# Reading the moving columns of the float32r matmuls from two halves in turn, in a convolution and feed-forward kernel

## The chip, the cores and the metric

The kernel runs on one core of one Trainium2 chip. The metric is the device time of one execution in microseconds (us). A core has five engines with queues of their own: TensorE (PE; its weight loads are shown apart as PEld), VectorE (DVE), ScalarE (ACT), GpSimd (POOL) and SyncE (SP). PE reads its operands from SBUF and adds its results up in PSUM; ACT and DVE read PSUM.

## The reference

A causal convolution of 7 taps along the sequence, with one softmax-normalized set of taps for each of 8 groups of 24 channels, then a feed-forward layer:

```python
w = softmax(weight)                       # (8 heads, 7 taps)
out[b, s, h, g] = sum_k w[h, k] * x_pad[b, s + k, h, g]   # x: (8, 4096, 192), 6 zeros in front
x = out.reshape(32768, 192)
h = x @ w_in                              # (192, 2048)
g = where(h >= 1, h, where(h <= -1, 0, (h + 1)**2 / 4))
return g @ w_out                          # (2048, 192)
```

Everything is float32, and the result has float32 precision.

## The kernel before

The 32,768 tokens go in 64 blocks of 512, numbered from 0. `d_ff` goes in 8 pairs of two 128-wide slices. A unit `q` is one pair of one block, so there are 512 units; `s, j = divmod(q, 8)`. Channels and `d_ff` stand on partitions, tokens in the free dimension.

For each unit PE first runs the products of `mm1` (line 440): the activations are the moving operand (512 tokens), the weights the stationary one, and the sum `h` (two PSUM banks of 512 tokens) has the tokens in the order of the moving columns. ACT then makes relu and square (lines 552, 553), DVE the min and max against `h` (line 878), and ACT a rounded copy `gh` in float32r (line 563); DVE makes the rest `gl = g - gh` and the sum `gt` of its two slices (lines 569, 575). Three units later PE runs `mm2` (line 501), with `gh`, `gl` and `gt` as the moving operand, into four PSUM banks `accr0`, `accr1`, `accm0`, `accm1`, which add up over the 8 units of a block.

Block 0 uses float32 for both layers; block 1 uses float32r for the first layer and float32 for the second (`mm2_first`, line 473, where `g` is the stationary operand). From block 2 on, both layers are made of three float32r products each (high times high, low times high, high times low). The very last unit is float32 again in its second layer (`pair_last`, line 650).

The contraction is cut into 64-row halves. Every product is issued as two matmuls, one on partitions 0 to 63 and one on 64 to 127, which run beside each other. A float32r unit has 9 such pairs in `mm1` and 9 in `mm2`, 36 matmuls of 64 rows x 512 columns.

At the end of a block `evac_banks` (line 593) copies the four banks to SBUF on ACT (line 599), in the order `accr0`, `accr1`, `accm0`, `accm1`. Each bank has one buffer, so the next block's `mm2` cannot start in a bank before its copy is done. Adding the four copies (`evac_add`, POOL's DMA queue, line 608), a transpose on DVE and the stores (`store`, line 610, SP's queue) follow later. The last block has its own copies (`evac_last`, line 635), split over ACT and DVE in halves of 256 tokens.

The order of the work on every engine is the order of the code: the schedule is written out by hand, in the main loop at the end of the function.

Of the kernel before, what the change touches and what calls it, by code (L numbers as in the profile page):

```python
# [8 lines left out]
F32 = mybir.dt.float32  # L9
# [9 lines left out]
P = 128  # L19
TB = 512  # L20
# [11 lines left out]
def lightconv_then_ffn(ctx: ExitStack, tc: tile.TileContext, x, weight, w_in, w_out, out):  # L32
# [24 lines left out]
    nc = tc.nc  # L57
    B, S, D = x.shape
# [11 lines left out]
    HALVES = (TOP, BOT)  # L70
# [6 lines left out]
    ob = ctx.enter_context(tc.tile_pool(name="ob", bufs=2))  # L77
# [359 lines left out]
    NQ = NSB * NPAIR  # L437
    hs, g32, gs, ghs, gls, gts, accs = {}, {}, {}, {}, {}, {}, {}

    def mm1(q):  # L440

        s, j = divmod(q, NPAIR)

        if q == 0:
            h = hs[q] = [ps_o.tile([P, TB], F32, name=n) for n in ("accr1", "accm0")]
        else:
            h = hs[q] = ps_h.tile([P, 2, TB], F32, name="h")
            h = [h[:, e, :] for e in range(2)]

        if q == 0:  # L450
            for e in range(2):
                nc.tensor.matmul(h[e], natural[:, e * P:(e + 1) * P], xop[s]["all"],  # L452
                                 start=True, stop=False)
            for e, half in enumerate(HALVES):
                nc.tensor.matmul(h[e], natural[half, CW:CI], xop[s]["r"][e],  # L455
                                 start=False, stop=True)
            return
        if s == 0:
            mms = [(WI[j], u + u, [xop[s][u]] * 2) for u in "nrs"]
        else:  # L460
            mms = [(W[j][:, part], u + u, [xop[s][u, x]] * 2) for u in "nsr"
                   for part, x in ((0, "hi"), (1, "hi"), (0, "lo"))]
        for n, (w, us, x) in enumerate(mms):
            for e in range(2):
                c0 = COL[us[e]][e]
                nc.tensor.matmul(h[e], w[HALVES[e], c0:c0 + P], x[e][e],  # L466
                                 start=(n == 0), stop=(n == len(mms) - 1))

    def new_accs(s):
        accs[s] = {(a, i): ps_o.tile([P, TB], F32, name=f"acc{a}{i}")  # L470
                   for a in "mr" for i in range(2)}

    def mm2_first(q):


        s, j = divmod(q, NPAIR)
        g, w = g32.pop(q), WF[j + LAG]
        if j == 0:
            new_accs(s)
        for e in range(2):  # L480
            for b in range(TB // P):
                a, c0 = "mr"[b // 2], b % 2 * D
                for i, half in enumerate(HALVES):
                    nc.tensor.matmul(accs[s][a, i][:, c0:c0 + D], g[half, e, b * P:(b + 1) * P],  # L484
                                     w[half, e, :], start=(j == 0 and e == 0 and b % 2 == 0),
                                     stop=(j == NPAIR - 1 and e == 1 and b % 2 == 1))

    XY, XZ, ZY = range(3)
# [5 lines left out]
    def leave(mm):  # L494
        nc.tensor.drain(fusable=True).then_inc(turns, 1)
        turn[0] += 1

    def enter():
        nc.tensor.wait_ge(turns, turn[0])

    def mm2(q):

        s, j = divmod(q, NPAIR)
        gh, gl, gt = ghs.pop(q), gls.pop(q), gts.pop(q)
        if j == 0:
            new_accs(s)
        wg, wl = WG[j], WL[j]
        low = {XY: gt, XZ: gl[:, 1, :], ZY: gl[:, 0, :]}
        seen = set()
        for k in range(9):  # L510
            for i, half in enumerate(HALVES):
                turned = k // 3 if j % 2 == 0 else 2 - k // 3
                bank, part = BANKS[i][turned], PARTS_OF[i][turned]
                w, g = ((wg[:, k % 3, part], gh[:, k % 3, :]) if k % 3 < 2
                        else (wl[:, part], low[part]))
                if i == 0 and k == 6:
                    enter()
                mm = nc.tensor.matmul(accs[s][bank], w[half], g[half],  # L518
                                      start=(j == 0 and bank not in seen),
                                      stop=(j == NPAIR - 1 and k % 3 == 2  # L520
                                            and (bank[0] == "m" or k == 8)
                                            or q == NQ - 2 and k % 3 == 2
                                            and (bank[0] == "m" or k == 8)))
                seen.add(bank)
                if i == 1 and k == 3:
                    leave(mm)
# [67 lines left out]
    def evac_banks(s):  # L594
        acc = accs.pop(s)
        t = {}
        for bank in (("r", 0), ("r", 1), ("m", 0), ("m", 1)):
            t[bank] = ob.tile([P, TB], F32, name="t", bufs=4)
            nc.scalar.copy(t[bank], acc[bank])
        sums[s, "m"], sums[s, "r"] = t["m", 0], t["r", 0]  # L600
        sums[s] = t

# [30 lines left out]
    last = {}  # L633

    def evac_last(s):

        acc = accs.pop(s)
        half, rest = slice(0, TB // 2), slice(TB // 2, TB)
        u, v, r = [ob.tile([P, TB], F32, name="t", bufs=4) for _ in range(3)]
        for n in (half, rest):  # L640
            nc.scalar.copy(u[:, n], acc["m", 0][:, n])
            nc.vector.tensor_tensor(out=v[:, n], in0=acc["m", 1][:, n], in1=u[:, n], op=ALU.add)
        for n in (half, rest):
            for to, a in ((TOP, 0), (BOT, 1)):
                nc.vector.tensor_tensor(out=v[to, n], in0=acc["r", a][to, n], in1=v[to, n],
                                        op=ALU.add)
                nc.scalar.copy(r[to, n], acc["r", 1 - a][to, n])
        last["m"], last["r"] = v, r

    def pair_last(q):  # L650

# [303 lines left out]
    for q in range(NQ + LATE):  # L955
        s, j = divmod(q, NPAIR)
        c, i = divmod(q, 2 * NPAIR)
# [8 lines left out]
        if c == 0 and i in (4, 5, 10):  # L966
            u = {4: "a", 5: "r", 10: "b"}[i]
# [7 lines left out]
        if q == NPAIR:  # L975
            mm2_first(done)
        if q < NQ:
            mm1(q)
        if done is not None and q != NPAIR:
            (pair_last if done == NQ - 1 else mm2 if done >= NF32 else mm2_first)(done)  # L980
# [21 lines left out]
        else:  # L1002
# [4 lines left out]
            if done is not None and done % NPAIR == NPAIR - 1 and done < NQ - 1:  # L1007
                (evac if done < NF32 else evac_banks)(done // NPAIR)
            if done == NQ - 2:
                evac_last(done // NPAIR)  # L1010
            if q == NF32:
                parts_lo(q)
            n = q - 1 if q < NF32 + 3 else q - 2
# [14 lines left out]
            if q < NQ:  # L1028
                if s > 2 and j in (3, 4):
                    evac_add(s - 1, j - 3)  # L1030
                if s <= 2 or s == NSB - 1:
                    m = 6 if s > 2 else 2
# [43 lines left out]
```

## Time and profile before

| | |
|---|---|
| device time, median of 3 runs | 2121.58 us (2121.57 to 2122.2) |
| profiled execution, first to last instruction (span) | 2120.2 us |
| PE busy | 2115.9 us (100% of the span) |
| ACT busy | 1976.6 us (93%) |
| DVE busy | 1975.6 us (93%) |
| POOL busy | 792.4 us (37%) |
| granted TensorE clock, mean over the span | 1.000 (of 2.4 GHz) |

The run times are some 1.4 us longer than the span, since they hold what lies around the first and the last instruction. Busy times of engines overlap. A matmul's row lasts from its start to the end of its last result, so rows of successive matmuls overlap; the rate of PE is read from the distance between starts.

### The profile page before, as it was taken

To read this page: it belongs to the slowest core of one execution; us is meant where nothing else is said; L and a number is where in the kernel's file an instruction comes from. 1 tells how busy PE (TensorE), PEld (TensorE's weight loads), DVE (VectorE), ACT (ScalarE), POOL (GpSimd) and SP (SyncE) were. 2 spreads that over 40 slices of the span, in tenths; PEclk is the share of its full clock that TensorE was granted. 3 is DMA by queue.
4 is the path that set the end of the run, shared out by engine and by line. 5 is a ranking of instruction groups with operands and counts; after the bars stand their busy time and mean duration, and the time that the engine had idled before them with its cause. 6 is when DMAs were issued, how large, how long until landed. Compare 5 with 4: busy or idle time off the path is not lost.

```text
span 2120.2 us, 46902 instructions
## 1 busy us (share of the span) xinstructions
PE 2115.9 (100%) x18644; PEld 1807.7 (85%) x18644; DVE 1975.6 (93%) x2109; ACT 1976.6 (93%) x2381; POOL 792.4 (37%) x749
## 2 busy tenths in 40 slices
PE   9999999999999999999999999999999999999999
PEld 6988888888888888888888888888888888888888
DVE  8899999999999999999999999999999999999997
ACT  7899999999999999999999999999999999999997
POOL 1534333343433433333333333343343333433331
PEclk9999999999999999999999999999999999999999
DMA  6333333433433434334333343343343433433322
GB/s 172 77 66 71 57 73 67 79 73 54 82 66 71 78 63 73 69 64 85 70 60 72 68 79 74 54 81 64 74 76 63 76 68 64 84 68 62 70 54 51
DMA packets 470685, 152.27 MB, mean 72 GB/s; under 512 B 418944, under 2 KB 426624, under 8 KB 470464
## 3 DMA queue, kind: packets, MB, share of 16 engines
q1 hardware_dynamic: 446880, 109.17, 24.7%
q0 software_dynamic: 23424, 39.99, 12.9%
q8 instruction: 146, 2.39, 0.5%
q14 instruction: 75, 0.61, 0.1%
q10 hardware_dynamic: 160, 0.10, 0.0%
HBM read 32.84 MB, written 25.17 MB: 27 GB/s over the span
## 4 chain that ended last, share of the span: by engine, by line
PE 100%; DVE 0%; issue 0%; POOL 0%; POOLq 0%; DVEq 0%
PE h L466 49%; PE accr L518 32%; PE accm L518 16%; PE accm L484 1%; PE accr L484 1%; PE accr L214 0%; PE accm L721 0%; PE accm L193 0%; PE h L664 0%; PE accm L664 0%; PE h L171 0%; PE accr L452 0%; PE accr L455 0%; PE accr L767 0%; PE accm L452 0%; PE accm L171 0%
## 5 line engine op out<-in xcount | busy, mean ns | idle before, releaser
L569 DVE TENSOR_TENSOR gl<-g,gh 128x1024 fp32r<-128x1024 f32 x495 | 742.8, 1501 | 63.4 <-ACT gh L563 58.5
L466 PE MATMUL h<-hi,w 64*128 64x512 f32 x4032 | 629.9, 387 | 0.0
L518 PE MATMUL accr<-gh,wg 64*128 64x512 f32 x3960 | 616.5, 386 | 0.0
L878 DVE SCALAR_TENSOR_TENSOR g<-g,h 128x1024 f32<-128x1024 f32 x504 | 607.8, 1206 | 6.9 <-ACT g L553 5.0
L552 ACT ACTIVATE g<-h 128x1024 f32<-128x1024 f32 (+1 forms) x497 | 509.9, 1026 | 99.5 <-PE h L466 97.4
L553 ACT ACTIVATE g<-g 128x1024 f32<-128x1024 f32 (+1 forms) x497 | 527.4, 1061 | 15.8
L563 ACT CAST gh<-g 128x1024 fp32r<-128x1024 f32 x495 | 516.7, 1044 | 0.5 <-DVE g L878 0.4
L129 POOL TENSOR_TENSOR y<-y,p 128x512 f32<-128x512 f32 x180 | 233.5, 1297 | 607.2 <-ACT p L237 413.0
L466 PEld LDWEIGHTS h<-hi,w 64*128 64x128 f32 x4032 | 391.8, 184 | 64.7 <-DVE g L878 0.2
L518 PEld LDWEIGHTS accr<-gh,wg 64*128 64x128 f32 x3960 | 384.2, 184 | 64.6
L129 POOL TENSOR_TENSOR r<-r,p 128x512 f32<-128x512 f32 x180 | 233.6, 1298 | 510.4 <-ACT p L237 363.7
L466 PE MATMUL h<-lo,w 64*128 64x512 f32 x2016 | 399.9, 386 | 0.0
L518 PE MATMUL accr<-gl,words 64*128 64x512 f32 x1980 | 392.1, 386 | 0.0
L575 DVE TENSOR_TENSOR m<-gl 128x512 fp32r<-128x512 f32 x495 | 336.1, 679 | 20.5 <-DVE gl L569 0.5
L518 PE MATMUL accm<-gh,wg 64*128 64x512 f32 x1980 | 308.3, 386 | 0.0
L466 PE MATMUL h<-rhi,w 64*128 64x512 f32 x992 | 303.9, 386 | 0.0
L466 PE MATMUL h<-rh,w 64*128 64x512 f32 x992 | 303.9, 386 | 0.0
L608 POOL DMA_DIRECT2D t<-t x244 | 206.3, 985 | 93.1 <-DMA t<-t 69.9
L466 PEld LDWEIGHTS h<-lo,w 64*128 64x128 f32 x2016 | 196.2, 184 | 32.3
L518 PEld LDWEIGHTS accr<-gl,words 64*128 64x128 f32 x1980 | 192.1, 184 | 32.3
L518 PEld LDWEIGHTS accm<-gh,wg 64*128 64x128 f32 x1980 | 192.1, 184 | 32.3
L466 PEld LDWEIGHTS h<-rhi,w 64*128 64x128 f32 x992 | 182.5, 184 | 16.2
(161 smaller groups left out, 2322.2 us busy)
## 6 DMA issues: line engine op xcount, KB each, us to landing
t<-t POOLq DMA_DIRECT2D x183, 128.0 KB, 3.7
out_dram<-osb SPq DMA_DIRECT2D x366, 64.0 KB, 1.9
raw<-in_x_dram SPq DMA_DIRECT2D x334, 68.0 KB, 2.4
hi<-hi SPq DMA_DIRECT2D x128, 128.0 KB, 2.8
lo<-lo SPq DMA_DIRECT2D x126, 128.0 KB, 3.1
t<-t POOLq DMA_DIRECT2D x61, 256.0 KB, 3.3
rhi<-rh SPq DMA_DIRECT2D x62, 128.0 KB, 3.5
rlo<-rl SPq DMA_DIRECT2D x62, 128.0 KB, 2.4
```

The lines of the kernel that those rows point to most:

```text
L129: add = nc.gpsimd.tensor_add(out, a, b)
L466: nc.tensor.matmul(h[e], w[HALVES[e], c0:c0 + P], x[e][e], start=(n == 0), stop=(n == len(mms) - 1))
L484: nc.tensor.matmul(accs[s][a, i][:, c0:c0 + D], g[half, e, b * P:(b + 1) * P], w[half, e, :], start=(j == 0 and e == 0 and b % 2 == 0), st ...
L518: mm = nc.tensor.matmul(accs[s][bank], w[half], g[half], start=(j == 0 and bank not in seen), stop=(j == NPAIR - 1 and k % 3 == 2 and (ban ...
L552: nc.scalar.activation(g[:, e, :], hs[q][:, e, :], AF.Relu, bias=0.5, scale=0.5)
L553: nc.scalar.activation(g[:, e, :], g[:, e, :], AF.Square)
L563: nc.scalar.copy(gh[:, e, :], gs[q][:, e, :])
L569: nc.vector.tensor_sub(gl[:, e, :], g[:, e, :], gh[:, e, :])
L575: return nc.vector.tensor_add(gt, gl[:, 0, :], gl[:, 1, :])
L608: nc.gpsimd.dma_start(out=to, in_=src, accum_op=ALU.add)
L878: nc.vector.scalar_tensor_tensor(out=g, in0=g, scalar=1.0, in1=h, op0=ALU.min, op1=ALU.max)
```

## The change

In `mm1` (blocks 1 to 63, but for the last unit) and in `mm2` the moving operand's access pattern is `p (a b) -> p b a` with `a=2`: the columns are read as 0, 256, 1, 257, and so on. A matmul still has 512 columns and writes its 512 results side by side. So `h` holds token `256 a + b` at place `2 b + a`; `gh`, `gl` and `gt` keep that order, and `mm2` applies the same reading once more. In the four banks a place `4 r + 2 b + a` then holds token `256 b + 128 a + r`.

The copies put the tokens back: for `accr0` and `accm0` ACT reads PSUM with a step of four elements and writes side by side; for `accr1` and `accm1` it reads side by side and writes to four places 128 elements apart in turn. `evac_last` reads the banks with a step of four elements on ACT and DVE. In block 1 the second layer takes its stationary blocks of `g` with a step of two elements.

```diff
+    def in_turn(t):
+        return t.rearrange("p (a b) -> p b a", a=2)
+    def by_token(t):
+        return t.rearrange("p (r b a) -> p b a r", b=2, a=2)
     def mm1(q):
+        seen = (lambda t: t) if s == 0 or q == NQ - 1 else in_turn
...
-                nc.tensor.matmul(h[e], w[HALVES[e], c0:c0 + P], x[e][e],
+                nc.tensor.matmul(h[e], w[HALVES[e], c0:c0 + P], seen(x[e][e]),
     def mm2_first(q):
...
-                    nc.tensor.matmul(accs[s][a, i][:, c0:c0 + D], g[half, e, b * P:(b + 1) * P],
-                                     w[half, e, :], start=(j == 0 and e == 0 and b % 2 == 0),
+                    block = (g[half, e, b * P:(b + 1) * P] if s == 0 else
+                             g[half, e].rearrange("p (k i a) -> p k a i", k=2, a=2)[:, b % 2, b // 2])
+                    nc.tensor.matmul(accs[s][a, i][:, c0:c0 + D], block, w[half, e, :], start=(j == 0 and e == 0 and b % 2 == 0),
     def mm2(q):
...
-                mm = nc.tensor.matmul(accs[s][bank], w[half], g[half],
+                mm = nc.tensor.matmul(accs[s][bank], w[half], in_turn(g[half]),
     def evac_banks(s):
...
-            nc.scalar.copy(t[bank], acc[bank])
+            if bank[1] == 0:
+                nc.scalar.copy(t[bank].rearrange("p (b a r) -> p b a r", b=2, a=2),
+                               by_token(acc[bank]))
+            else:
+                nc.scalar.copy(t[bank].rearrange("p (b a r) -> p r b a", b=2, a=2),
+                               acc[bank].rearrange("p (r b a) -> p r b a", b=2, a=2))
     def evac_last(s):
-        half, rest = slice(0, TB // 2), slice(TB // 2, TB)
-        u, v, r = [ob.tile([P, TB], F32, name="t", bufs=4) for _ in range(3)]
-        for n in (half, rest):
+        parts = [ob.tile([P, TB], F32, name="t", bufs=4) for _ in range(3)]
+        u, v, r = [t.rearrange("p (b a r) -> p b a r", b=2, a=2) for t in parts]
+        acc = {k: by_token(t) for k, t in acc.items()}
+        for n in range(2):
...
```

No engine issues an instruction more or less, and none changes its place. What differs is the shape of every second copy. ACT's queue at the end of block 2, before (`t` is the copy in SBUF, `acc..` the PSUM banks, `h` and `g` the tiles of the unit beside it):

```order
L552 ACTIVATE g_1740<-h_1701 128x1024
L553 ACTIVATE g_1740<-g_1740 128x1024
L599 COPY t_1743<-accr0_1329 128x512
L599 COPY t_1745<-accr1_1330 128x512
L599 COPY t_1747<-accm0_1327 128x512
L599 COPY t_1749<-accm1_1328 128x512
L563 CAST gh_1756<-g_1687 128x1024
```

The same place in the changed kernel:

```order
L562 ACTIVATE g_1740<-h_1701 128x1024
L563 ACTIVATE g_1740<-g_1740 128x1024
L610 COPY t_1743<-accr0_1329 128x512
L613 COPY t_1745<-accr1_1330 128x128x4
L610 COPY t_1747<-accm0_1327 128x512
L613 COPY t_1749<-accm1_1328 128x128x4
L573 CAST gh_1756<-g_1687 128x1024
```

Only line numbers and the written shape of `accr1` and `accm1` differ; the four copies stand where they stood, ahead of the next unit's rounded copy.

## Rows read from the trace of the kernel before

**Rows 1.** The page: busy us of each engine, and the chain that ended last.

```profile
PE 2115.9 (100%) x18644; PEld 1807.7 (85%) x18644; DVE 1975.6 (93%) x2109; ACT 1976.6 (93%) x2381; POOL 792.4 (37%) x749
...
PE 100%; DVE 0%; issue 0%; POOL 0%; POOLq 0%; DVEq 0%
```

**Rows 2.** Engines' busy us (and instructions) in 16 units: us, PE, PEld, DVE, ACT, POOL.

```profile
500.00:565.28 65.28, 65.28 (x578) 55.87 (x576) 61.28 (x64) 61.70 (x75) 24.86 (x22) 1.00 0.39 71
1000.00:1065.28 65.28, 65.28 (x578) 55.87 (x576) 61.27 (x64) 61.71 (x74) 24.86 (x22) 1.00 0.38 70
```

**Rows 3.** The chain in order of time: start us, us, what.

```profile
126.17 2.04 PE h L466 x18
128.21 0.68 PE accr L518 x6
128.89 0.68 PE accm L518 x6
...
130.25 2.04 PE h L466 x18
...
166.97 2.04 PE h L466 x18
```

**Rows 4.** Timeline of PE in block 0, float32: start us, us, engine, line, tiles, shape, count.

```profile
14.88 1.02 PE L466 MATMUL h<-hi,gh 64*128 64x512 f32 x4
...
20.03 0.82 PE L484 MATMUL accm<-wf,g 64*128 64x192 f32 x8
20.68 0.82 PE L484 MATMUL accr<-wf,g 64*128 64x192 f32 x8
21.33 0.82 PE L484 MATMUL accm<-wf,g 64*128 64x192 f32 x8
21.98 0.82 PE L484 MATMUL accr<-wf,g 64*128 64x192 f32 x8
22.63 1.02 PE L466 MATMUL h<-hi,gh 64*128 64x512 f32 x4
```

**Rows 5.** Groups by line and shape: busy us, mean ns; idle before, its releaser.

```profile
L466 PE MATMUL h<-hi,w 64*128 64x512 f32 x4032 | 629.9, 387 | 0.0
L518 PE MATMUL accr<-gh,wg 64*128 64x512 f32 x3960 | 616.5, 386 | 0.0
L563 ACT CAST gh<-g 128x1024 fp32r<-128x1024 f32 x495 | 516.7, 1044 | 0.5 <-DVE g L878 0.4
L599 ACT COPY t<-accm 128x512 f32<-128x512 f32 x122 | 66.9, 612 | 0.0
L599 ACT COPY t<-accr 128x512 f32<-128x512 f32 x122 | 65.6, 590 | 0.0
L484 PEld LDWEIGHTS accm<-wf,g 64*128 64x128 f32 x256 | 23.4, 186 | 2.7 <-issue 2.2 <-DVE warm L139 0.2 <-DVE g L878 0.2
L366 ACT ACTIVATE m<-words 128x384 f32<-128x384 f32 x8 | 4.4, 550 | 0.0
L366 ACT ACTIVATE m<-words 128x768 f32<-128x768 f32 x4 | 3.7, 918 | 0.3 <-DMA words<-in_moe_w_out_dram 0.3
```

**Rows 6.** Timeline of all engines at the end of a block.

```profile
1011.36 0.62 PE L466 MATMUL h<-hi,w 64*128 64x512 f32 x4
1011.56 1.08 ACT L599 COPY t<-accr 128x512 f32<-128x512 f32 x2
...
1012.52 1.10 ACT L599 COPY t<-accm 128x512 f32<-128x512 f32 x2
...
1013.40 0.62 PE L518 MATMUL accr<-gh,wg 64*128 64x512 f32 x4
...
1014.08 0.62 PE L518 MATMUL accm<-gh,wg 64*128 64x512 f32 x4
```

**Rows 7.** Who waited for whom: us in total, times, longest us.

```profile
ACT g L552 <- PE h L466: 97.4, 219, 1.1
...
ACT t L641 <- PE accm L518: 2.7, 1, 2.7
```

More of the change, by code (lines that the diff above doesn't have):

```diff
@@ L637, in evac_last @@
         acc = accs.pop(s)
-        half, rest = slice(0, TB // 2), slice(TB // 2, TB)
-        u, v, r = [ob.tile([P, TB], F32, name="t", bufs=4) for _ in range(3)]
-        for n in (half, rest):
+        parts = [ob.tile([P, TB], F32, name="t", bufs=4) for _ in range(3)]
+        u, v, r = [t.rearrange("p (b a r) -> p b a r", b=2, a=2) for t in parts]
+        acc = {k: by_token(t) for k, t in acc.items()}
+        for n in range(2):
             nc.scalar.copy(u[:, n], acc["m", 0][:, n])
             nc.vector.tensor_tensor(out=v[:, n], in0=acc["m", 1][:, n], in1=u[:, n], op=ALU.add)
-        for n in (half, rest):
+        for n in range(2):
             for to, a in ((TOP, 0), (BOT, 1)):
@@ L647, in evac_last @@
                 nc.scalar.copy(r[to, n], acc["r", 1 - a][to, n])
-        last["m"], last["r"] = v, r
+        last["m"], last["r"] = parts[1], parts[2]
     def pair_last(q):
```

## The prediction

> **What bounds the kernel now.** I read the page first. PE is busy for the whole span, and the chain that ended last is PE alone [rows 1]. ACT and DVE stand close behind: a stretch of 16 units takes 65.28 us, and in it ACT is busy for 61.70 and 61.71 us, DVE for 61.28 and 61.27 [rows 2]. The waits say which side is late: ACT waits for PE's `h`, 97.4 us in all, and no large wait goes the other way [rows 7]. So the time is PE's rate, with some 5% of room before ACT, and 6% before DVE.
>
> The chain in order of time gives the rate. Ten units lie between the starts 126.17 and 166.97 [rows 3], so one takes 4.080 us. A unit has 18 pairs of matmuls (one of each pair per row half, side by side), which makes 226.7 ns a pair; the pieces of 9 pairs (2.04 us) and of 3 pairs (0.68 us) agree with that to the last digit, in `mm1` and `mm2` alike. Whatever holds the pairs at 226.7 ns does not depend on what ACT, DVE or the DMA do just then.
>
> Is that the floor? Block 0 does the same kind of products in float32. There 12 pairs of 512 columns start at 14.88 and end where the next group starts, at 20.03: 429.2 ns a pair. The 16 pairs of 192 columns after them take 2.60 us: 162.5 ns a pair [rows 4]. The two give a slope of (429.2 - 162.5) / 320 = 0.833 ns a column, two cycles at the granted 2.4 GHz, and 2.5 ns that depend on no column. A float32r pair at one cycle a column would be 512 x 0.4167 + 2.5 = 215.8 ns by the same account. It takes 10.8 ns more. The pair's 226.7 ns are 544 cycles for 512 columns, 17/16. The row halves, the bank writes and the number of rows are the same in both, so the excess belongs to float32r: either to reading columns at one a cycle, or to the start of such a matmul.
>
> **The change part by part.** How many pairs it touches: the row of `hi` in `mm1` has 4,032 matmuls, 8 to a unit, so 504 units; the last unit keeps its order, which leaves 503 x 9 = 4,527 pairs. In `mm2` the row of `gh` to `accr` has 3,960, 8 to a unit, so 495 units and 4,455 pairs [rows 5]. Together 8,982 pairs, 8,982 x 0.2267 = 2,036 us of the 2,120.2.
>
> *The reading order.* No row shows a moving operand with a step, so I bound it. [...] Above, the nearest row is the float32 pair, whose columns enter at half the rate: 429.2 ns. [...] Fully hidden: 8,982 x 10.8 ns = 97 us. Half hidden: 49 us.
>
> [...]
>
> *What is late next.* At 215.8 ns PE needs 288 x 0.2158 = 62.16 us for 16 units. ACT needs 61.71 plus what the copies gain. So PE stops being the only bound: two engines with 62.2 us of work each, which hand tiles to each other through two `h` buffers, and DVE with 61.3. They can't both be full. I take 63.2 us for the stretch, an estimate of mine (1.6% above the larger of the two). The 495 units that have both layers in float32r make 30.9 such stretches. The gain is then 30.9 x 2.08 = 64 us; with all of ACT's slack used it would be 30.9 x 3.08 = 95 us.
>
> *The copies of the banks.* 244 of them, at 590 and 612 ns [rows 5], 8 in 16 units. From 512 to 1,024 columns ACT goes from 612 to 1,044 ns, 0.844 ns a column, side by side. With a step of two elements it goes from 550 ns at 384 columns to 918 at 768, 0.958 ns a column [rows 5]. That is 0.06 us more on 512 columns, the lower bound and the value I take, since the step of two is the only stepped read of ACT in the rows. The upper bound is half the rate, 0.43 us more. The cover: the copies to `accr` end at 1012.64, 0.76 us ahead of the first matmul that needs the bank, at 1013.40; those of `accm` end at 1013.62, 0.46 us ahead of 1014.08 [rows 6]. Four copies may grow by 0.46 us together, 0.115 us each, before PE waits. At 0.06 us each nothing waits, and ACT's stretch grows to 62.2 us, which is in the sum above. They cannot become shorter: the columns are as many.
>
> *The rest.* In block 1, 128 weight loads of `mm2_first` read with a step of two, 64 pairs; a load takes 186 ns [rows 5] and lies beside a pair of 162.5 ns [rows 4]. Twice as long would be 64 x 0.19 = 12 us, the upper bound; I take nothing, because it reads 128 columns only and two elements lie close together. In `evac_last`, 12 operations on 256 columns get a step of four; if each lost 256 x 0.844 = 0.22 us and eight stood on the path, 1.7 us; I take 0.2.
>
> The sum against the profiled 2,120.2: 2,120.2 - 64 + 0.2 = 2,056 us, and 1.4 us around the span make 2,058. With half of the pause hidden PE remains the bound (16 units in 63.7 us) and it is 2,120.2 - 49 + 1.6 = 2,073. Between these I say 2,060.
>
> **The rivals.** *No change.* The 10.8 ns are the start of a float32r matmul and hang on no column. For it: they are the same everywhere, and the trace has only one width of float32r. Against it: the float32 pairs start at 2.5 ns, with the same loads of 128 weight columns. Then PE keeps 226.7 ns, the copies stay under their cover, and the time is 2,121.6 with a microsecond or two about it.
>
> *The copies take over: slower.* Place: the first matmuls of `mm2` in each block. If ACT takes stepped elements at half the rate, four copies grow by 1.73 us; above the 0.46 us of cover PE waits 1.27 us in each of 61 blocks, 77 us: 2,199. It decides from 0.115 us a copy on. If the columns are faster at the same time, ACT with 61.71 + 8 x 0.43 = 65.2 us becomes the bound and the time is near 2,120 to 2,150. For it: no row shows a step of four from PSUM, nor writes 128 elements apart. Against it: a step of two cost ACT an eighth.
>
> *The columns enter at half the rate: much slower.* If each column needs a read of its own that takes two cycles, a pair takes what the float32 pair takes, 429.2 ns, and the change costs 8,982 x 0.2025 = 1,819 us: 3,941. [...]
>
> **How the numbers follow.** Faster columns: 0.55, with 2,027 (ACT full) to 2,100 (a quarter hidden) as its own range. No change: 0.16. Copies take over: 0.11. Half the rate: 0.18. Times within 0.2% (some 4 us) of before can't be told from no change. The range of 2,027 to 2,200 holds the first three, 0.82; what it leaves out is the last. Faster 0.55, same 0.16, slower 0.29.
>
> **What would show it.** Right: starts of pairs in `mm1` and `mm2` 216 to 221 ns apart, PE's chain now broken by waits for DVE's `g` or ACT's `gh`, ACT busy above 97% of a stretch, copies under 0.7 us. Wrong: pairs still at 226.7 (first rival); a wait of PE for the copies at each block's first `mm2` (second); pairs above 226.7 (third). Copies of two lengths would tell stepped reads from scattered writes.

## The result, and the profile after

The changed kernel takes 2085.01 us (median of 4 runs, 2084.51 to 2085.29) against 2121.57 before: a ratio of 0.9827, 95% interval 0.9813 to 0.9841. It is faster by 36.6 us, where 62 were forecast. The profiled execution spans 2,082.7 us, 37.5 less than before.

First the page, busy us of each engine, against [rows 1]:

```profile
PE 2062.0 (99%) x18644; PEld 1937.3 (93%) x18644; DVE 1957.2 (94%) x2109; ACT 2009.4 (96%) x2381; POOL 789.2 (38%) x749
...
PE 52%; ACT 21%; DVE 17%; issue 9%; DVEq 0%; ACTq 0%; POOL 0%; POOLq 0%
```

The chain that was PE alone now goes through ACT and DVE for 38% of the span, and ACT's busy time has grown by 33 us although it does the same work. The chain in order of time (start us, us, what) shows PE where nothing holds it, against [rows 3]:

```profile
500.13 0.65 PE accr L528 x6
500.78 1.94 PE h L475 x18
502.72 0.65 PE accr L528 x6
503.37 0.65 PE accm L528 x6
504.01 0.65 PE accr L528 x6
504.66 1.94 PE h L475 x18
```

From 500.78 to 504.66 is 3.88 us for a unit, 215.6 ns a pair at the two digits of the view (the starts themselves are 215.8 ns apart), where it was 226.7. So PE has the whole of the 10.8 ns, 97 us on 8,982 pairs. Adding up, over all float32r pairs, by how much each starts later than 215.8 ns after the one before gives 60 us: 97 - 60 is the gain that was measured. The waits (us in total, times, longest us) say where these 60 us go, against [rows 7]:

```profile
PEld accm L528 <- ACT t L613: 38.9, 61, 0.8
...
ACT g L562 <- PE h L475: 29.2, 67, 0.8
PEld h L475 <- DVE g L894: 24.8, 73, 0.7
...
PE accm L528 <- ACT t L613: 14.4, 49, 0.5
```

These rows can't be added up: the wait of the matmul on `accm` (14.4 us) lies within that of its weight load (38.9 us), and the two together cover 39 us. PE waits for the copies of the banks in each of the 61 blocks, and in 73 units for DVE to free an `h` buffer; neither wait was there before. By the late starts, 42 of the 60 us are lost in `mm2` and 18 in `mm1`. The copies by line and shape (busy us, mean ns), against [rows 5]:

```profile
L613 ACT COPY t<-accr 128x512 f32<-128x512 f32 x61 | 66.7, 1094 | 0.0
L613 ACT COPY t<-accm 128x512 f32<-128x512 f32 x61 | 65.9, 1080 | 0.0
L610 ACT COPY t<-accm 128x512 f32<-128x512 f32 x61 | 39.6, 650 | 0.0
L610 ACT COPY t<-accr 128x512 f32<-128x512 f32 x61 | 34.7, 569 | 0.0
```

Line 610 reads PSUM with a step of four and costs what a plain copy cost, 569 and 650 ns against 590 and 612. Line 613 reads side by side and scatters its writes over four places: 1,094 and 1,080 ns. The end of a block in the timeline (start us, us), against [rows 6]:

```profile
512.55 0.57 ACT L610 COPY t<-accr 128x512 f32<-128x512 f32 x1
...
513.01 1.09 ACT L613 COPY t<-accr 128x512 f32<-128x512 f32 x1
...
513.88 0.65 ACT L610 COPY t<-accm 128x512 f32<-128x512 f32 x1
...
514.42 1.08 ACT L613 COPY t<-accm 128x512 f32<-128x512 f32 x1
...
514.92 0.38 PE L528 MATMUL accm<-gh,wg 64*128 64x512 f32 x1
...
515.55 0.70 PE L528 MATMUL accm<-gh,wg 64*128 64x512 f32 x3 [0.25 <-ACT t L613]
```

The last copy ends at 515.50. The matmuls on `accr` had started at 514.27; the first on `accm1` could have gone beside the one at 514.92, and starts at 515.55, some 0.6 us late.

### The profile page after: what moved, and what is told of

Its sections match the earlier page's. It is cut to its first block, busy times and chain, and to the rows that moved or that the text cites. A ratio compares the mean times of both kernels' runs of the same rounds, so it can differ in the third digit from the quotient of the medians.

```text
span 2082.7 us, 46902 instructions
## 1 busy us (share of the span) xinstructions
PE 2062.0 (99%) x18644; PEld 1937.3 (93%) x18644; DVE 1957.2 (94%) x2109; ACT 2009.4 (96%) x2381; POOL 789.2 (38%) x749
## 4 chain that ended last, share of the span: by engine, by line
PE 52%; ACT 21%; DVE 17%; issue 9%; DVEq 0%; ACTq 0%; POOL 0%; POOLq 0%
PE h L475 27%; PE accr L528 14%; PE accm L528 8%; DVE gl L579 7%; DVE g L894 6%; ACT g L562 5%; ACT gh L573 4%; ACT t L613 4%; ACT t L610 3%; ACT g L563 2%; DVE m L585 2%; DVE osb L635 1%; ACT p L237 1%; PE accm L495 1%; PE accr L495 1%
## 5 line engine op out<-in xcount | busy, mean ns | idle before, releaser
L528 PE MATMUL accr<-gh,wg 64*128 64x512 f32 x3960 | 675.9, 378 | 0.0
L475 PEld LDWEIGHTS h<-hi,w 64*128 64x128 f32 x4032 | 461.6, 186 | 36.4 <-DVE g L894 24.8
L528 PE MATMUL accr<-gl,words 64*128 64x512 f32 x1980 | 455.9, 376 | 0.0
L475 PE MATMUL h<-lo,w 64*128 64x512 f32 x2016 | 455.1, 376 | 0.0
L528 PEld LDWEIGHTS accr<-gh,wg 64*128 64x128 f32 x3960 | 435.2, 185 | 19.9 <-ACT t L613 0.3
L528 PE MATMUL accm<-gh,wg 64*128 64x512 f32 x1980 | 359.8, 382 | 14.6 <-ACT t L613 14.4
L528 PEld LDWEIGHTS accm<-gh,wg 64*128 64x128 f32 x1980 | 239.9, 186 | 42.5 <-ACT t L613 38.9
L528 PEld LDWEIGHTS accr<-gl,words 64*128 64x128 f32 x1980 | 267.8, 186 | 3.7
L475 PEld LDWEIGHTS h<-lo,w 64*128 64x128 f32 x2016 | 263.6, 186 | 6.0
L528 PE MATMUL accm<-m,words 64*128 64x512 f32 x990 | 237.7, 378 | 0.0
```

The lines of the kernel that those rows point to most:

```text
L475: nc.tensor.matmul(h[e], w[HALVES[e], c0:c0 + P], seen(x[e][e]), start=(n == 0), stop=(n == len(mms) - 1))
L528: mm = nc.tensor.matmul(accs[s][bank], w[half], in_turn(g[half]), start=(j == 0 and bank not in seen), stop=(j == NPAIR - 1 and k % 3 == 2 ...
```

## The experiments

**Theory:** the columns have their full gain, and most of what is missing is lost at the two scattered copies. **Rival:** ACT, DVE and PE with some 62 us of work each in 16 units cannot go faster together, and the wait for the copies only shows where that comes out. A second question is why reading in turn is faster at all.

### All four copies as stepped reads

In place of the two forms, for every bank:

```diff
-            if bank[1] == 0:
...
+            nc.scalar.copy(t[bank].rearrange("p (b a r) -> p b a r", b=2, a=2),
+                           by_token(acc[bank]))
```

> The columns as in the changed kernel; all four copies of a block's banks read PSUM with a step of four elements and write side by side (the accr0/accm0 form), none scatters its writes. Theory: the changed kernel's PE has its full gain (215.8 ns a pair) and gives back some 53 us waiting for the two scattered copies (1.09 us each against 0.57 to 0.65). Then PE's waits for copies go from 53 us to under 5, ACT loses about 1.0 us a block, and the time is 2030 to 2045 us. Rival: ACT, DVE and PE with some 62 us of work each per 16 units are what sets the time, and the wait only moves to another place: 2060 to 2080.

Measured: 2046.89 us (2045.87 to 2047.65), 0.9647 of before (0.9634 to 0.966). That is 38 us less than the changed kernel, and 2 us above the theory's range, which had taken the waits for the copies at 53 us by adding the two rows that overlap (38.9 and 14.4). The copies and the waits of this kernel:

```profile
L609 ACT COPY t<-accm 128x512 f32<-128x512 f32 x122 | 66.2, 603 | 0.0
L609 ACT COPY t<-accr 128x512 f32<-128x512 f32 x122 | 64.4, 579 | 0.0
```

```profile
ACT g L562 <- PE h L475: 39.6, 80, 1.0
PEld h L475 <- DVE g L890: 27.9, 78, 0.5
```

No wait of PE for a copy is left; the wait for DVE to free `h` stays as it was. PE's starts are late by 23 us in sum instead of 60 (17 in `mm1`, 6 in `mm2`), and 97 - 23 = 74 us is what the span lost (2,120.2 to 2,045.8). The theory holds, and the rival is refuted as the main cause. This version beats both kernels.

### The copies alone

The kernel before with the changed kernel's four copies and nothing else; the columns are read in order, so the output's tokens are shuffled.

> The kernel before with only its four copies per block changed to those of the changed kernel; columns are read in order, so the tokens of the output are shuffled. Theory: the scattered copies take 1.09 us by themselves, the four grow by 1.0 us, 0.46 us of it under cover, and PE waits about 0.5 us in each of 61 blocks: 2145 to 2155. Rival: they are slow only beside a PE that reads its columns in turn; then they take 0.6 us here and the time stays at 2121.

Measured: 2160.33 us, 1.0183 of before (1.0169 to 1.0197); 5 us above the theory's range. In this kernel's profile, the copies and PE's waits:

```profile
L607 ACT COPY t<-accr 128x512 f32<-128x512 f32 x61 | 67.8, 1112 | 0.0
L607 ACT COPY t<-accm 128x512 f32<-128x512 f32 x61 | 66.3, 1087 | 0.0
```

```profile
PEld accm L522 <- ACT t L607: 35.4, 61, 0.6
```

The scattered copies are as long beside a PE that reads in order, so their length is their own and does not come from the order in which PE reads. By themselves they cost 39 us. That the cost is at the writes, not at the reads, follows from the two forms side by side: the one with steps in PSUM (line 604) takes 573 and 654 ns here, where plain copies took 590 and 612. Whether the distance of the four places or the short run of four makes the writes slow was not tried.

### No reordering at all

The changed kernel with plain copies, so the output's tokens are shuffled:

```diff
+            nc.scalar.copy(t[bank], acc[bank])
```

> The changed kernel with plain copies of the four banks, side by side on both ends, so the tokens of the output are shuffled. Theory (a step of four elements costs ACT nothing when it reads PSUM): the same as with four stepped copies, 2047 within 4 us, copies at 0.58 to 0.61 us. Rival (the step costs some of ACT's time in ways the copies' own length doesn't show): 2030 to 2042.

Measured: 2047.13 us, 0.9648 of before (0.9635 to 0.9661), the same as with four stepped reads; the copies take 605 and 578 ns, with stepped reads 603 and 579. Reading PSUM with a step of four costs ACT nothing that can be measured here.

### The first layer alone

`mm2` reads in order; all copies read PSUM with a step of two.

```diff
-                mm = nc.tensor.matmul(accs[s][bank], w[half], in_turn(g[half]),
+                mm = nc.tensor.matmul(accs[s][bank], w[half], g[half],
...
+            nc.scalar.copy(t[bank].rearrange("p (a b) -> p a b", a=2), by_token(acc[bank]))
```

> The changed kernel with only the first layer's columns in turn; the second layer reads in order, and all four copies (and the last block's) read PSUM with a step of two elements and write side by side. Theory (the gain is 10.8 ns for each pair that is changed, and below PE's rate of 63.7 us in 16 units nothing else binds): 4,527 pairs, 49 us, 2072 to 2078. Rival (PE's waits for DVE to free h eat half of it, as 18 us of PE's time went there in the changed kernel): 2085 to 2100.

Measured: 2081.6 us, 0.9811 of before (0.9797 to 0.9824): 40 us less, between the two expectations. PE waits for no copy, and for DVE's `g` once, 0.4 us. But its starts are 9 us late in sum, all of it at the start of `mm2` in each unit, after the change from one order to the other: its first three distances are 235, 232 and 231 ns instead of 226.7. That is some 17 ns a unit, and 49 - 9 is the gain. Two units in the chain, with the slower first piece behind each change (0.70 us instead of 0.68):

```profile
500.30 1.94 PE h L475 x18
502.25 0.70 PE accr L528 x6
502.94 0.68 PE accm L528 x6
503.62 0.68 PE accr L528 x6
504.30 1.94 PE h L475 x18
506.25 0.70 PE accr L528 x6
```

What these 17 ns are was not tried.

### Which orders are fast

Two kernels, each with the first layer of every block in another order (their outputs are not the reference's), show the distance between successive starts on a row half.

```diff
+                nc.tensor.matmul(h[e], w[HALVES[e], c0:c0 + P], PATTERNS[k](x[e][e]),
```

> The kernel before, but the first layer of block s reads its moving columns in pattern s mod 16 (the output is not the reference's): 0 in order; 1, 2, 3, 4 from 2, 4, 8, 16 parts in turn; 5, 6, 7 with a step of 2, 4, 16; 8, 9, 10 from two halves in turn in runs of 2, 8, 16; 11, 12 two neighbouring stretches of 4 and of 16 columns in turn; 13 each of 256 columns twice; 14 two matmuls of 256 columns; 15 one of 384 and one of 128. The distance between the starts of pairs is read for each. Theory A (pause at the end of each 16 columns of one stream): 1 to 4 at 215.8; steps of 2 to 16 above 226.7; 11 and 12 between; 13 about 221 (half as many ends); 256 columns in order 113.3 ns. Theory B (cost of neighbouring columns in succession): steps of 2 and more, and 11, 12 at 215.8; runs of 8 and 16 near 226.7. Theory C (a fixed 10.8 ns start that a stepped pattern happens to avoid): 256 columns in order take 120 ns, and every stepped pattern 215.8, 8 to 10 included.

> As the earlier kernel of patterns (first layer of block s, output not the reference's), with other patterns by s mod 14: 0 in order; 1 the pairs 0 1, 1 2, 2 3, ...; 2, 3, 4, 5 two in turn at a distance of 2, 8, 32, 128; 6 from two halves in turn, in each first the even, then the odd places; 7 four in turn at a distance of 4; 8, 9 each column four and eight times; 10 one column 512 times; 11 a step of 8; 12, 13 two halves in turn in runs of 4 and 64. Theory (innermost loop of two, whatever the distance): 2 to 5 at 215.8, 1 too, 6 as well; 7 near 283 as four in turn from quarters took. Rival (memory: two reads in succession must not fall on neighbours of one line): 1 and 2 above 226.7 and 8, 9, 10 too, 3 to 5 at 215.8. Second rival (what counts is that each of the two streams goes on by one column): 6 far above 226.7, 2 to 5 at 215.8.

Measured, read from the starts in the traces (one run of each kernel; only the distances are used of them):

```
order of the moving columns                                    ns a pair
in order                                                       226.7
two in turn, 256, 128, 32, 16, 8 or 4 apart                    215.8
0 1, 1 2, 2 3, ... ; each column twice, four, eight times      215.8
one column 512 times                                           217
two in turn, 2 apart (0 2 1 3 4 6 5 7 ...)                     226.7
two halves in turn, in each first the even places              226.7
two halves in turn in runs of 2 / 4 / 8 / 16 / 64              340 / 250 / 245 / 240 / 227
four in turn, from quarters / 4 apart                          283 / 268
8 / 16 parts in turn                                           487 / 432
a single stream with a step of 2 / 4 / 8 / 16                  451 / 460 / 432 / 432
```

Two blocks of the second kernel that follow each other, in the chain of waits (start us, us; 9 pairs in each piece of `h`): two in turn 128 apart up to 212, then the halves' even places first:

```profile
210.11 1.94 PE h L499 x18
212.06 0.70 PE accr L551 x6
212.75 0.68 PE accm L551 x6
213.43 0.68 PE accr L551 x6
214.11 2.04 PE h L499 x18
...
218.19 2.04 PE h L499 x18
```

And in the first kernel, a single stream with a step of two:

```profile
240.19 4.08 PE h L490 x18
```

What this says of the three theories. The fixed start: where weights were loaded ahead, at a unit's first pair, 256 columns in order take 113.3 ns and 384 take 171.0; 17/16 gives 113.3 and 170.0, a fixed 10.8 ns gives 120 and 173.3. So the excess goes with the columns. (The later pairs of 256 columns are 120 ns apart, and so are their weight loads; they do not decide.) This theory also expected 215.8 of every stepped pattern, and most took longer. The cost of neighbours: steps of 2 to 16 should have been free and take twice as long (432 to 460 ns); the pairs 0 1, 1 2 are neighbours and are fast (215.8). It falls. The pause of a single stream, hidden by a second one: it fits two halves in turn (215.8) and the runs of 64 (227), but it expected 215.8 from 4, 8 and 16 parts as well, which took 283, 487 and 432, a time in between for stretches of 4 and 16 columns, which took 215.8, and 221 for a column read twice, which took 215.8; and it does not give the twofold cost of a step. So it does not hold as a rule either; what is left of it is that the excess of the plain order goes with the columns.

Of the second kernel's three, the innermost loop of two fails at 2 apart and at the halves' even places (226.7 both); the rival on neighbours read in succession fails at 0 1, 1 2 and at columns read four and eight times (215.8); and the second rival expected the halves' even places far above 226.7 and 2 apart at 215.8, where both took 226.7.

### Two orders that undo themselves

Both are their own inverse, so that with the same order in both layers the copies stay plain:

```diff
+        return t.rearrange("p (d a b) -> p d b a", a=2, b=2)     # 0 2 1 3 4 6 5 7 ...
+        return t.rearrange("p (a b c) -> p c b a", a=2, c=2)     # 0 256 2 258 ... 1 257 ...
```

> The kernel before, with the moving columns of both float32r layers (from block 2 on) read as 0, 2, 1, 3, 4, 6, 5, 7, ...: the innermost loop has two columns, two places apart. Read so in both layers the tokens are back in order by themselves, so every copy is that of the kernel before. Theory (an innermost loop of two columns is what removes the 10.8 ns, at any distance): pairs at 215.8 ns, and a time of 2040 to 2050, that of the kernel with four stepped copies or a little less. Rival (the two streams have to lie in different stretches of memory; 4, 16 and 256 apart were enough, 2 are not): pairs at 226.7 ns or above, 2121 or more.

> The kernel before, with the moving columns of both float32r layers (from block 2 on) read as 0, 256, 2, 258, ..., 254, 510, 1, 257, 3, 259, ..., 255, 511: two halves in turn, in each first the even places. Read so twice the tokens are back in order, so all copies are those of the kernel before. In the kernel of near patterns this order ran at 215.8 ns a pair. Theory (what the changed kernel loses against 2024 us beside PE's waits for its scattered copies is PE's wait for DVE to free h): the same as with four stepped copies, 2043 to 2050, with PE's waits for copies under 5 us. Rival (the stepped copies still cost): 2030 to 2038.

Measured: 2121.43 us, ratio 1.0 (0.9991 to 1.0009), and 2121.48 us, 0.9999 (0.999 to 1.0008). Both kernels run at 226.7 ns a pair. The chain of the first and of the second, one unit each:

```profile
501.00 2.04 PE h L471 x18
503.04 0.68 PE accr L523 x6
...
505.08 2.04 PE h L471 x18
```

```profile
501.54 2.04 PE h L471 x18
503.57 0.68 PE accr L523 x6
...
505.62 2.04 PE h L471 x18
```

The first refutes the idea that an innermost loop of two columns is enough. The second rested on a misreading of mine, and what its expectation says of the earlier kernel is wrong: there, this order stood right behind two in turn 128 apart, has the same counts in its access pattern, and was taken for the same; the rows at 214.11 and 218.19 above show 2.04 us.

A third way back to plain copies takes a second layer that reads evens, then odds:

```diff
+                mm = nc.tensor.matmul(accs[s][bank], w[half], evens_odds(g[half]),
```

> First layer as in the changed kernel (0, 256, 1, 257, ...); the second layer reads its moving columns as all even places, then all odd ones, which puts the tokens back in order inside the matmuls, so the copies and the last block's copies are those of the kernel before. Theory A (a pause whenever a stream of neighbouring columns leaves a stretch of memory, hidden by a second stream): evens then odds is one stream that leaves stretches twice as often, so mm2's pairs take more than 226.7 ns, up to 240, and the time is 2090 to 2160. Theory B (neighbouring columns one after the other are what costs): mm2's pairs are at 215.8 as well, and with plain copies the time is 2025 to 2040.

Measured: 3077.44 us, 1.4504 of before (1.4484 to 1.4524). `mm2`'s pairs are 451 ns apart, far beyond what theory A gave, and theory B falls. One unit in the chain, the first layer at its fast rate and 3 pairs of `mm2` in each piece of 1.35 us:

```profile
505.44 1.95 PE h L475 x18
507.39 1.36 PE accr L528 x6
508.75 1.35 PE accm L528 x6
510.10 1.35 PE accr L528 x6
511.46 1.95 PE h L475 x18
```

### Does DVE hold the rest?

> The changed kernel with four stepped copies (2047), and the sum of gl's two slices (0.68 us on DVE) given to POOL in every fourth unit. Theory (of the 97 us that 8,982 pairs of 10.8 ns make, 23 are still lost to PE's waits for DVE to free h, since DVE is 96% busy): DVE loses 2.7 us in 16 units, PE's wait for h falls from 28 us to under 12, the time is 2026 to 2038. Rival (ACT, as busy as DVE, holds the units back, or POOL's sums are late): 2045 to 2080.

```diff
+        eng = nc.gpsimd if q % 4 == 1 else nc.vector
+        return eng.tensor_add(gt, gl[:, 0, :], gl[:, 1, :])
```

Measured: 2067.04 us, 0.9741 of before (0.9728 to 0.9754), 20 us slower than with the sums on DVE. DVE's and POOL's sums in this kernel:

```profile
L586 DVE TENSOR_TENSOR m<-gl 128x512 fp32r<-128x512 f32 x371 | 312.3, 842 | 15.3 <-DVE gl L579 0.9
...
L586 POOL TENSOR_TENSOR m<-gl 128x512 fp32r<-128x512 f32 x124 | 183.7, 1482 | 279.9 <-DVE gl L579 279.9
```

The mean of 842 ns (703 without the edit) hides two kinds: 311 of the sums left to DVE take 677 ns, as nearly all do without the edit, and 60 take 1.7 us on average, against 10 such sums without it. Each of the 60 runs beside an addition or a subtraction of POOL's own (lines 129 and 272). With that DVE's busy time falls by 13 us only (1,965.4 to 1,952.8). The waits of this kernel:

```profile
PEld h L475 <- DVE g L891: 31.3, 97, 0.8
PEld accm L528 <- DVE m L586: 26.4, 29, 1.7
```

The wait for `h` does not fall (31.3 against 27.9), and the wait of `mm2` for DVE's sums has grown from 8.1 to 26.4 us; 26 of its 29 stand behind one of the long sums. By PE's late starts, `mm1` loses 18 us as it did (17), and `mm2` 26 instead of 6: these are the 20 us. So the rival was right about the time, and its sums are late, but mostly those on DVE (the wait for POOL's own is 7.6 us). Why DVE's sums are long beside POOL was not tried. Whether less work on DVE would give the 23 us back stays open: this edit did not take much away. The same edit on top of the order with swapped ends told nothing on it, since PE was the bound there:

> As the kernel with the swapped ends, with the sum of gl's two slices (0.68 us on DVE) given to POOL in every fourth unit. Theory (DVE is now what holds PE, with 63 us of work in 65.28): DVE loses 2.7 us in 16 units, PE's wait for h falls from about 28 us to under 10, and the time is 2025 to 2038. Rival (ACT, with the same load, is what holds the units, or POOL's sums come late because of its other work): 2045 to 2080.

Measured: 2122.65 us, 1.0004 of before (0.9995 to 1.0013).

## Why the prediction was right, and where it was off

*PE bounds the kernel, and 226.7 ns is not its floor:* right. The float32 pairs of block 0 gave the estimate of 215.8 ns, and the changed pairs stand on it; none of the orders tried is faster.

*The reading order:* right in size (all of the 10.8 ns, 97 us on 8,982 pairs), and 17/16 of the columns is near at 256 and 384 columns too (113.3 and 171.0 ns). The terms of a pause fully, half or a quarter hidden were an estimate of the author's: no run shows a pause that a second stream hides; what the runs show in its place is that pairs read in order are 226.7 ns apart and pairs with two halves in turn 215.8. If a second stream hid one, four, eight and sixteen parts in turn should have been as fast, and they took 283, 487 and 432 ns. That the one order chosen is among the fast ones was in part luck: no row of before shows a moving operand read in turn. The half-rate rival had no place here, but it was no fancy: a step of two in a single stream does run at 451 ns.

*What is late next:* the estimate of 63.2 us for 16 units was near. With copies of plain length they take 62.9 us (units of 3.932 us on average), 0.75 us above PE's own 62.16; over the span 23 us are lost so, where 33 (97 - 64) had been allowed. The wait that PE then has is the one named, for DVE's `g`, through the two `h` buffers.

*The copies of the banks:* the step that failed. One value, 0.06 us more on 512 columns from ACT's read with a step of two, was taken for both forms. The stepped reads cost nothing (579 and 603 ns with all four so, against 590 and 612 before); the scattered writes cost 0.50 and 0.47 us each, beyond the upper bound of 0.43. So four copies grew by about 1.0 us where 0.46 was covered, and PE waits 39 us for them; without them the kernel is 38 us faster. This is the second rival's place and mechanism with its price halved, since half of the copies have the slow form; it took from the gain instead of turning it over, because the columns did become faster. The sum without that wait is what the kernel with four stepped reads shows: 2,047, where 2,058 to 2,073 were worked out.

*The sum:* the prediction had 97 us of gain, 33 less for engines that hand tiles to each other, and nothing less for the copies: 64. The runs show 97, less 23, less 38: 36. The two misses have opposite signs, so the time came out nearer to the forecast than the account of the copies alone would have it, and it lies well inside a range that reached to 2,200 because the second rival was in it.

*The rest:* the 12 stepped operations of the last block and the 128 weight loads don't show: with four stepped reads, gain and lost time add up to the span within 1 us.

## What to carry to other kernels

Compare the distance between matmul starts with that of another product of the same kernel before calling PE full: "100% busy" here held 10.8 ns of 226.7 that a reading order could take away. When PE gets faster, the work that was just covered decides: size each new form of a copy by itself, a stepped read and a scattered write are not one edit with one price. Of two ways to permute while copying from PSUM, here the read side was free (579 and 603 ns against 590 and 612) and the write side nearly doubled the copy (1,094 and 1,080 ns).

## What the runs showed of the hardware that was not expected

The rate of these kernels' float32r matmuls went with the order of their moving columns over a factor of more than two: 215.8 ns a pair with two columns in turn 4, 8, 16, 32, 128 or 256 apart, 226.7 in order, 268 to 283 with four in turn, 432 to 460 with a single stream of steps 2 to 16, 487 with eight parts in turn. Two columns in turn 2 apart were no faster than in order (226.7), and two streams that each go on in steps of two were not either (226.7). No one rule that was tried explains all of these, and the cause stays open. ACT writing to four places 512 bytes apart in turn took 1.08 to 1.11 us for 512 columns, against 0.57 to 0.65 with any of the other forms.
